# Attention scores in two PSUM tiles of two banks instead of one of four, with the order of all work made anew

## Chip, cores and metric

One core of a Trainium2 chip. The metric is device microseconds (us) of one launch. The kernel before was timed three times: 781.19, 783.55 and 784.84 us, median 783.55 us.

## What is computed

Causal attention in blocks of 64 (4 batches, 8 heads, 576 positions, head size 64), then two feed-forward layers over the 2304 tokens. Cut to what matters:

```
scores = scale * np.matmul(q, k.transpose(0, 1, 3, 2))
scores = np.where(block_i >= block_j, scores, -1e9)
attn = softmax(scores)
x = np.matmul(attn, v)                       # 2304 x 512 after the transpose of heads
h = x @ w_in;  g = np.maximum(h, 0.0) + np.log1p(np.exp(-np.abs(h)));  x = g @ w_out       # 512 -> 2048 -> 512
h = x @ w_in2; solu = h * softmax(h); x = layernorm(solu) * g_ln @ w_out2                  # 512 -> 1024 -> 512
```

## The kernel before

Each large product is made of three matmuls in a fast float type: both operands are split into a high and a low part, and high x high, high x low and low x high are added up in PSUM.

**The work comes in five kinds of items.** `UnitA` is attention for the first 256 queries of two heads (16 units, at the start). `UnitC` is attention from query 256 on for two heads (16 units, one after another; called a unit below). `Piece` converts weights. `Pair` takes two of the 16 column blocks of the first layer for 256 tokens: 24 matmuls into `hp` (tasks `a`), three ACT functions and a few DVE operations, then 24 matmuls into `acc` (tasks `b`). `Tok` is the second layer for 128 tokens. Pairs of one group of tokens run between the units of the next, so that PE has work while a unit waits for its softmax.

**The order is planned.** A unit's tasks are handed to `Plan.add` with an engine, a duration, a rank and the tasks that must come first. `Plan.run` goes through the plan's own time and gives each engine the ready task of lowest rank; the tables `OFF` and `RANK` are numbers added to the ranks. Tasks that two engines can do (`{"ACT": ..., "DVE": ...}`) go to the one that would end sooner. What comes out is one fixed list of instructions for each engine and for the DMA queue of SP; on the chip each engine takes its list in order.

**Two kinds of waits.** The plan's dependencies only set the order. The waits that the chip obeys are put in afterwards by the tile layer, which goes through that order and makes an access to a PSUM tile wait for the accesses of other engines to the same tile that stand before it, whether or not they touch the same banks.

**A unit's scores** lie in the tile `S`, four banks of 512 columns (line 821). `mm_both` writes the scores of 128 queries of both heads into banks 0 and 1 (i = 0, 384 keys) and of the next 128 into banks 2 and 3 (i = 1, 512 keys). DVE masks each half (`mask`, L467) and reduces it to its maxima (`max`, L472); ACT takes the exponentials head by head (`exp`, L481): twice into `eC0`, twice into `eC1`. Then `mm_qk(2)` writes the last 64 queries (576 keys, 288 columns a bank) into banks 0 and 1 again, and one more maximum and exponential follow. Each exponential is cut into 16-bit halves (`split`, tile `hl`), transposed by DMA (`tr`), and put together by DVE (`merge`, L522). The product with v (`pv`) of a unit runs in the middle of the next unit: `tail` puts it behind an exponential of that unit, into bank 3, which `exp(1, 1)`, the first of the two on `eC1`, has read out. `scale` (L538) multiplies it by the reciprocal sums, which come back from DRAM in `rC`. All matmuls stand at line 238.

```
mm01 = add("PE", 1614, 0.0, self.mm_both, [self.t_ql] + ...)
self.t_mm = t = add("PE", 797, r, partial(self.mm_qk, 2), [mm01, self.t_exp[0, 0], self.t_exp[0, 1]])
p1.tail([self.t_exp[1, 1]])
```

Of the kernel before, what the change touches and what calls it, by code (L numbers as in the profile page):

```python
# [10 lines left out]
F32 = mybir.dt.float32  # L11
# [9 lines left out]


OFF = {
    "Pair.a": -354.9, "Pair.abs": 39459.0, "Pair.b": 18236.7, "Pair.do_gh": 216226.0, "Pair.do_gl": 13257.7,
    "Pair.evac": -82948.2, "Pair.exp": -117702.0, "Pair.ln": -30665.3, "Pair.store": -79781.5, "Pair.stt": -62739.8,
    "Piece.bits0": -100434.0, "Piece.bits0@P0": -27714.9, "Piece.bits1": 65312.7, "Piece.bits1@P0": -101077.0,
    "Piece.do_hi": -19168.6, "Piece.do_hi@P0": -29991.6, "Piece.do_hi_g": -10835.1, "Piece.do_lo": 62401.8,
    "Piece.do_lo@P": -122217.0, "Piece.do_lo@P0": -16882.1, "Piece.do_lo_g": -33281.2, "Piece.load": 61438.7,
    "Piece.load@P0": -221951.0, "Piece.signed": -4876.1, "Piece.signed@P0": -103215.0, "Tok.a": -132718.0,
    "Tok.aggr": 7517.3, "Tok.bm": 58620.7, "Tok.center": -11408.7, "Tok.exp": -45235.8, "Tok.ln_hi": 28283.8,  # L30
    "Tok.ln_lo": 116041.0, "Tok.load": -268344.0, "Tok.logexp": -134098.0, "Tok.max": -65917.9,
    "Tok.merge": -135054.0, "Tok.mul": 52834.8, "Tok.o_evac": 47450.1, "Tok.small1": 71861.5, "Tok.small2": -55930.6,
    "Tok.split": -4685.6, "Tok.split_hi": 24778.5, "Tok.split_lo": -127140.0, "Tok.stats": 68934.5,
    "Tok.store": 157613.0, "Tok.tr": -45442.3, "Tok.x_hi": -107660.0, "Tok.x_lo": -20156.8, "UnitA.copy": -193390.0,
# [15 lines left out]
    "UnitC.den2": 65738.1, "UnitC.exp": 104667.0, "UnitC.load_qk": -83707.0, "UnitC.load_v": -36917.0,  # L50
    "UnitC.mask": -89564.7, "UnitC.max": -78960.5, "UnitC.merge": 54501.7, "UnitC.merge4": 149992.0,
    "UnitC.mm_both": -120396.0, "UnitC.mm_qk": -21356.3, "UnitC.norm": 76221.3, "UnitC.pv": -31503.3,
    "UnitC.qk_hi": -189467.0, "UnitC.qk_lo": -5389.2, "UnitC.rs_load": 138338.0, "UnitC.rs_store": -59470.7,
    "UnitC.scale": -44805.3, "UnitC.split": 94027.7, "UnitC.tr": -223984.0, "UnitC.x_hi": 131467.0,
    "UnitC.x_lo": 10651.6, "UnitC.xx": -154207.0,
}
RANK = {
# [3 lines left out]
    "Tok": (611105.0, 4133.14),  # L61
}
MARGIN = {
    "PE": 600.0, "ACT": 100.0, "DVE": 100.0, "POOL": 100.0,
# [2 lines left out]
B, H, S, D = 4, 8, 576, 64  # L67
# [4 lines left out]
NB = S - NA  # L72

QA = (slice(0, 128), slice(128, 384))
MASKED = -8.0e9
BANKS = (slice(0, 2), slice(2, 4), slice(0, 2))

WC = (384, 512, 576)

# [136 lines left out]
def dve_ns(n, per=1.04):  # L216
    return 70.0 + per * n
# [11 lines left out]
def body(ctx: ExitStack, tc: tile.TileContext, qk, qkA, vP, vA, w1, w2, u1, u2, gln, out):  # L229
    nc = tc.nc  # L230
    PE, ACT, DVE, POOL, SP = nc.tensor, nc.scalar, nc.vector, nc.gpsimd, nc.sync
# [5 lines left out]
    def mm(out, lhsT, rhs, start, stop):  # L237
        PE.matmul(out, lhsT, rhs, start=start, stop=stop, skip_group_check=True)  # L238
# [9 lines left out]
    def at_of(lst, i):  # L248
        return lst[i] if 0 <= i < len(lst) else None
# [16 lines left out]
    state = {}  # L266
# [90 lines left out]
    class UnitC:  # L357
# [6 lines left out]
        def plan(self, prev, opened):  # L364
            p1, p2 = at_of(prev, len(prev) - 1), at_of(prev, len(prev) - 2)
# [9 lines left out]
            for i, w in enumerate(WC):  # L375
                r, heads = 7.0 * i, ((0, 1), (1, 0), (0,))[i]
                if i < 2:
                    t = add("DVE", 140, r, partial(self.mask, i), [mm01])
                else:
                    self.t_mm = t = add("PE", 797, r, partial(self.mm_qk, 2), [mm01, self.t_exp[0, 0], self.t_exp[0, 1]])  # L380
                t = add("DVE", dve_ns(w * len(heads)), r, partial(self.max, i), [t])
                e = []
                for j in heads:
                    e.append(add("ACT", 250 + .833 * w, r, partial(self.exp, i, j), [t] + e + (p1.t_mg[i] if p1 else [])))
                    self.t_exp[i, j] = e[-1]
                if i == 1 and p1:
                    p1.tail([self.t_exp[1, 1]])
                cols, back = w * len(heads), [p1.t_tr[i]] if p1 else []
                n = [add({"ACT": 100 + .833 * cols, "DVE": 75 + .52 * cols}, None, r, partial(self.split, i, k), e + back) for k in range(2)]
                self.t_tr[i] = add("SP", 300 + 1.6 * cols, r, partial(self.tr, i), n, 2600.0)  # L390
# [54 lines left out]

        def scores(self, i):

            return state["S"][:, BANKS[i], 0:WC[i] if i < 2 else WC[2] // 2]

        def mm_qk(self, i):  # L450
            S, w = self.scores(i), WC[i]
# [74 lines left out]
            copy(e, state["p4"].bitcast(U16)[64 * j:64 * j + 64].rearrange("p (q two) -> p q two", two=2), src)  # L526

        def pv(self):
            o, ps = state["S"][:, 3], state["ps"]
            for t in range(4):  # L530
                q0 = 0 if t < 3 else 128
                for j in range(2):
                    mm(o[64 * j:64 * j + 64, q0:NB], self.v[:, 256 * j + 64 * t:256 * j + 64 * t + 64], ps[:, t, j, q0:NB], t == 0, False)
            mm(o[:, 256:NB], self.v[:, 512:640], state["p4"], False, True)

        def scale(self):
            self.xn = self.r
            DVE.tensor_mul(self.xn, state["S"][:, 3, 0:NB], self.r)  # L538

        def x_hi(self, c, off, done, w, e):  # L540
            copy(e, xt_of(c)[:, 0, self.pr, off:off + w], self.xn[:, done:done + w])
# [274 lines left out]
    def open_b():  # L816
        right[0].close()
        right[0] = ExitStack()
        state["pat"] = right[0].enter_context(pool("atB", "right"))
        q = right[0].enter_context(pool("qaB", "right", space=PSUM))  # L820
        state["S"] = q.tile([128, 4, 512], F32, name="S")
        state["dC"] = [[state["pat"].tile([128, 32], F32, name=f"d{x}{i}") for x in "CT"] for i in range(2)]
        for d, _ in state["dC"]:
            DVE.memset(d, 1.0)
        state["eC"] = [state["pat"].tile([128, 2 if i < 2 else 1, w], F32, name=f"eC{i}") for i, w in enumerate((WC[0], WC[1], WC[2] + 64))]
        state["hl"] = [state["pat"].tile([128, (2 * w if i < 2 else w + 64)], F32, name=f"hl{i}") for i, w in enumerate(WC)]
        DVE.memset(state["hl"][2], 0.0)
        state["ps"] = state["pat"].tile([128, 4, 2, NB], F32, name="ps")
        state["p4"] = state["pat"].tile([128, 64], F32, name="p4")
# [323 lines left out]
```

## Time and profile before

| | |
|---|---|
| median of three runs | 783.55 us |
| the profiled execution, and its span | 784.22 us, 782.4 us |
| mean granted PE clock | 0.985 of full |
| PE busy with matmuls | 735.1 us, 94% of the span |
| weight loads (beside matmuls) | 652.5 us, 83% |
| DVE, ACT, POOL busy | 592.7 us (76%), 409.8 us (52%), 0.7 us |
| DMA | 95.00 MB, 121 GB/s |

The profiled execution is 1.8 us longer than its span (what lies around the instructions) and 0.7 us over the median. Unless a text says otherwise, places are in us from the start of the span. The 16 units run from 191.9 us, the first matmul into `S`, to 464 us, the last; the units are numbered 0 to 15 by their start.

### The profile page before, as it was taken

How to read it: one execution, taken by the hardware profiler on the slowest of the kernel's cores; microseconds unless marked ns; L12 is line 12 of the kernel's file. 1: busy time of each engine (PE TensorE's matmuls, PEld its weight loads, DVE VectorE, ACT ScalarE, POOL GpSimd, SP SyncE). 2: the span in 40 equal slices, each digit the busy share in tenths (PEclk: the TensorE clock that was granted, in tenths of full speed). 3: DMA queues.
4: the chain of work that ended last, by engine and by line, in shares of the span. 5: the costliest groups of instructions: out<-in, count | busy, mean ns of one | idle time of the engine just before them, and what ended most of it. 6: DMA issues, size and time to landing. Idle time of an engine off the chain costs nothing.

```text
span 782.4 us, 13713 instructions
## 1 busy us (share of the span) xinstructions
PE 735.1 (94%) x5288; PEld 652.5 (83%) x5288; DVE 592.7 (76%) x1232; ACT 409.8 (52%) x877; POOL 0.7 (0%) x6
## 2 busy tenths in 40 slices
PE   7899999999898988898898899999999999999998
PEld 4688989999877777777887699999999888888887
DVE  6899995565777876777888755634698998989883
ACT  5787855563765666655665645543454342233231
POOL 0000000000000000000000000000000000000000
PEclk9899999999999998999999999999999999999999
DMA  7665742223666665566876552302513524443233
GB/s 258 197 196 182 227 149 68 69 42 88 138 135 148 138 165 123 116 132 134 172 148 132 101 138 81 124 13 72 200 52 82 141 76 108 95 108 88 59 83 80
DMA packets 165216, 95.00 MB, mean 121 GB/s; under 512 B 134816, under 2 KB 148384, under 8 KB 165152
## 3 DMA queue, kind: packets, MB, share of 16 engines
q1 hardware_dynamic: 165152, 94.14, 47.9%
q8 instruction: 41, 0.67, 0.3%
q14 instruction: 23, 0.19, 0.1%
HBM read 51.91 MB, written 9.70 MB: 79 GB/s over the span
## 4 chain that ended last, share of the span: by engine, by line
PE 64%; DVE 18%; ACT 10%; DMA 4%; issue 3%; SPq 0%; ACTq 0%; DVEq 0%
PE hp L238 14%; PE acc L238 13%; PE op L238 13%; PE h L238 13%; PE S L238 8%; ACT eC L481 5%; DVE mC L472 4%; DMA raw<-in_w_dram 3%; PE R L238 2%; DVE ps L522 2%; DVE a L315 1%; DVE t L769 1%; DVE mA L627 1%; PE r L238 1%; ACT eA L636 1%
## 5 line engine op out<-in xcount | busy, mean ns | idle before, releaser
L238 PE MATMUL hp<-xt,w 128*128 128x256 f32 x1728 | 216.6, 282 | 0.4 <-DVE t L769 0.3
L238 PEld LDWEIGHTS hp<-xt,w 128*128 128x128 f32 x1728 | 207.7, 190 | 6.9 <-issue 5.2
L238 PE MATMUL acc<-gh,w 128*128 128x256 f32 x768 | 144.8, 281 | 0.5 <-ACT gh L244 0.5
L238 PEld LDWEIGHTS acc<-gh,w 128*128 128x128 f32 x768 | 121.4, 189 | 3.0 <-issue 2.1
L238 PE MATMUL acc<-gl,w 128*128 128x256 f32 x384 | 107.6, 280 | 1.8 <-DVE gl L777 1.7
L238 PE MATMUL h<-u,w 128*128 128x512 f32 x432 | 100.2, 389 | 0.0
L238 PE MATMUL op<-w,w2w 128*128 128x512 f32 (+1 forms) x456 | 100.0, 378 | 0.0
L238 PEld LDWEIGHTS op<-w,w2w 128*128 128x128 f32 x456 | 82.5, 188 | 16.0
L238 PEld LDWEIGHTS h<-u,w 128*128 128x128 f32 x432 | 80.8, 188 | 16.6
L481 ACT ACTIVATE eC<-S,mC 128x384 f32<-128x384 f32 (+2 forms) x80 | 52.0, 653 | 61.0 <-DVE mC L472 26.9
L760 ACT ACTIVATE t<-hp 128x512 f32<-128x512 f32 x72 | 42.7, 593 | 66.1 <-PE hp L238 55.6
L769 DVE SCALAR_TENSOR_TENSOR t<-hp,t 128x512 f32<-128x512 f32 x72 | 49.1, 682 | 35.9 <-ACT t L766 35.5
L238 PEld LDWEIGHTS acc<-gl,w 128*128 128x128 f32 x384 | 72.1, 188 | 2.5 <-DVE gl L777 2.4
L238 PE MATMUL S<-ps,v 128*64 128x320 f32 (+1 forms) x256 | 38.8, 450 | 14.9 <-ACT eC L481 12.9
L1070 ACT ACTIVATE ob<-op,A 128x512 f32<-128x512 f32 (+1 forms) x19 | 12.6, 663 | 75.8 <-PE op L238 72.8
L777 DVE TENSOR_TENSOR gl<-t,gh 128x512 fp32r<-128x512 f32 x72 | 49.3, 684 | 2.0 <-ACT gh L244 0.7
L472 DVE TENSOR_REDUCE mC<-S 128x2 f32<-128x768 f32 (+2 forms) x48 | 45.4, 974 | 6.3 <-ACT eC L481 3.7
L238 PE MATMUL acc<-gh,w2w 128*128 128x256 f32 x256 | 48.4, 281 | 0.0
L766 ACT ACTIVATE t<-t 128x512 f32<-128x512 f32 x72 | 45.5, 632 | 1.4
L763 ACT ACTIVATE t<-t 128x512 f32<-128x512 f32 x72 | 45.6, 633 | 1.2
L522 DVE COPY ps<-eC 128x1536 uint16<-128x1536 uint16 (+2 forms) x48 | 45.2, 945 | 1.4 <-DMA eC<-hl 1.3
L238 PEld LDWEIGHTS S<-ps,v 128*64 128x64 f32 x256 | 18.5, 149 | 32.5 <-ACT eC L481 14.5
(175 smaller groups left out, 1086.0 us busy)
## 6 DMA issues: line engine op xcount, KB each, us to landing
raw<-in_w_dram SPq DMA_DIRECT2D x32, 512.0 KB, 4.7
qkC<-in_qk_dram SPq DMA_DIRECT2D x16, 480.0 KB
raw_u<-in_u_dram SPq DMA_DIRECT2D x11, 512.0 KB, 3.5
v<-in_vP_dram SPq DMA_DIRECT2D x16, 320.0 KB, 2.9
x2s<-stg SPq DMA_DIRECT2D x18, 256.0 KB, 2.8
xr<-x2s SPq DMA_DIRECT2D x18, 256.0 KB, 3.2
qkA<-in_qkA_dram SPq DMA_DIRECT2D x16, 256.0 KB, 4.0
out_dram<-ob SPq DMA_DIRECT2D x15, 256.0 KB, 2.2
```

Source lines behind the costliest of these rows:

```text
L238: PE.matmul(out, lhsT, rhs, start=start, stop=stop, skip_group_check=True)
L315: DVE.scalar_tensor_tensor(out=self.a, in0=self.raw[:, :, 0], scalar=29, in1=self.a, op0=ALU.logical_shift_right, op1=ALU.bitwise_or)
L472: DVE.tensor_reduce(out=self.m[:, i:4:2] if i < 2 else self.m[:, 4:5], in_=self.scores(i), axis=AX.X if i < 2 else AX.XY, op=ALU.max, nega ...
L481: ACT.activation(e, sc, AF.Exp, bias=self.m[:, c:c + 1], accum_out=self.den[:, d:d + 1])
L522: DVE.tensor_copy(dst, src)
L627: DVE.tensor_reduce(out=self.m[:, i, w * j:w * j + w], in_=st[:, :, QA[i]], axis=AX.X, op=ALU.max, negate=True)
L760: ACT.activation(self.t, self.hp, AF.Abs)
L763: ACT.activation(self.t, self.t, AF.Exp, scale=-1.0)
L766: ACT.activation(self.t, self.t, AF.Ln, bias=1.0)
L769: DVE.scalar_tensor_tensor(out=self.t, in0=self.hp, scalar=0.0, in1=self.t, op0=ALU.max, op1=ALU.add)
L777: DVE.tensor_sub(self.gl, self.t, self.gh)
L1070: ACT.activation(self.ob[:, cols], self.o[cols.start][:, cols], AF.Copy, scale=self.A)
```

## The change

The tile of four banks becomes a list of two tiles of two: scores i = 0 and 2 in `S0`, scores i = 1 and the product with v in `S1` (its second bank). The banks hold the same data as before. The product with v is put behind the last exponential on `S1`, `exp(1, 0)`, and not behind the first. All numbers of `OFF` and `RANK` are others, and so the order of the whole program is another. Units 8 to 15 of `UnitA` are transposed by DMA in both kernels.

```diff
 OFF = {
-    "Pair.a": -354.9, "Pair.abs": 39459.0, "Pair.b": 18236.7, "Pair.do_gh": 216226.0, "Pair.do_gl": 13257.7,
...
+    "Pair.a": 12428.5, "Pair.abs": -8234.6, "Pair.b": 41785.8, "Pair.do_gh": 285265.0, "Pair.do_gl": -45051.3,
...
-BANKS = (slice(0, 2), slice(2, 4), slice(0, 2))
...
                 if i == 1 and p1:
-                    p1.tail([self.t_exp[1, 1]])
+                    p1.tail([self.t_exp[1, 0]])
...
         def scores(self, i):
 
-            return state["S"][:, BANKS[i], 0:WC[i] if i < 2 else WC[2] // 2]
+            return state["S"][i % 2][:, :, 0:WC[i] if i < 2 else WC[2] // 2]
...
         def pv(self):
-            o, ps = state["S"][:, 3], state["ps"]
+            o, ps = state["S"][1][:, 1], state["ps"]
...
         def scale(self):
             self.xn = self.r
-            DVE.tensor_mul(self.xn, state["S"][:, 3, 0:NB], self.r)
+            DVE.tensor_mul(self.xn, state["S"][1][:, 1, 0:NB], self.r)
...
-        state["S"] = q.tile([128, 4, 512], F32, name="S")
+        state["S"] = [q.tile([128, 2, 512], F32, name=f"S{i}") for i in range(2)]
```

Two places of the order. PE in unit 11 (374.5 us in the trace), from the last matmul ahead of the product with v or the scores i = 2 on; `qkh` and `qkl` are the high and low parts of q and k, `ps` the transposed exponentials, `hp` a pair's tile. Before:

```order
L238 MATMUL acc_129<-gh_4172,w2_1_114 128x256
L238 MATMUL S_2315<-ps_2329,v_4274 64x320 x6
L238 MATMUL S_2315<-ps_2329,v_4274 64x192 x2
L238 MATMUL S_2315<-p4_2330,v_4274 128x64
L238 MATMUL S_2315<-qkh_4190 128x288 x2
L238 MATMUL S_2315<-qkl_4191,qkh_4190 128x288 x2
L238 MATMUL S_2315<-qkh_4190,qkl_4191 128x288 x2
L238 MATMUL hp0_130<-xt_2721,w1_8_105 128x256 x12
L238 MATMUL hp0_130<-xt_2721,w1_9_106 128x256 x12
```

And changed:

```order
L236 MATMUL acc_129<-gh_4173,w2_1_114 128x256
L236 MATMUL S0_2315<-qkh_4191 128x288 x2
L236 MATMUL S0_2315<-qkl_4192,qkh_4191 128x288 x2
L236 MATMUL S0_2315<-qkh_4191,qkl_4192 128x288 x2
L236 MATMUL S1_2316<-ps_2330,v_4253 64x320 x6
L236 MATMUL S1_2316<-ps_2330,v_4253 64x192 x2
L236 MATMUL S1_2316<-p4_2331,v_4253 128x64
L236 MATMUL hp0_130<-xt_2724,w1_8_105 128x256 x12
L236 MATMUL hp0_130<-xt_2724,w1_9_106 128x256 x12
```

The scores i = 2 moved ahead of the product with v. They stand in this order in all 15 units of the changed kernel that hold a product with v (unit 0 holds none); before, in 8 of the 15 (not in units 3, 8, 9, 11, 12, 14 and 15).

ACT in the same unit, from its first exponential on (`t` is a pair's tile, `hl` the halves for the transpose, `xt` the tokens for the pairs). Before:

```order
L481 ACTIVATE eC0_2322,dC1_2318<-S_2315,mC_4295 128x384 x2
L481 ACTIVATE eC1_2323,dC1_2318<-S_2315,mC_4295 128x512
L760 ACTIVATE t_4331<-hp1_131 128x512
L481 ACTIVATE eC1_2323,dC1_2318<-S_2315,mC_4295 128x512
L763 ACTIVATE t_4331<-t_4331 128x512
L244 ACTIVATE hl1_2326<-eC1_2323 128x1024
L766 ACTIVATE t_4331<-t_4331 128x512
L244 ACTIVATE xt_4049<-rC_4310 128x192
L481 ACTIVATE eC2_2324,dC1_2318<-S_2315,mC_4295 128x576
```

And changed:

```order
L479 ACTIVATE eC0_2323,dC1_2319<-S0_2315,mC_4296 128x384 x2
L479 ACTIVATE eC1_2324,dC1_2319<-S1_2316,mC_4296 128x512
L758 ACTIVATE t_4344<-hp1_131 128x512
L479 ACTIVATE eC1_2324,dC1_2319<-S1_2316,mC_4296 128x512
L761 ACTIVATE t_4344<-t_4344 128x512
L242 ACTIVATE hl1_2327<-eC1_2324 128x1024
L428 ACTIVATE qkh_4371<-qkC_4272 128x384
L429 ACTIVATE qkh_4371<-qkC_4272 128x576
L764 ACTIVATE t_4344<-t_4344 128x512
L479 ACTIVATE eC2_2325,dC1_2319<-S0_2315,mC_4296 128x576
```

The four exponentials stand as they stood; behind them the copies of the next q and k came to ACT, and the copy from `rC` went back behind the last exponential.

## Rows read from the trace of the kernel before

**Rows 1.** The page: span, and busy time of each engine.

```profile
span 782.4 us, 13713 instructions
PE 735.1 (94%) x5288; PEld 652.5 (83%) x5288; DVE 592.7 (76%) x1232; ACT 409.8 (52%) x877; POOL 0.7 (0%) x6
```

**Rows 2.** Busy time by stage; the columns stand in the first line.

```profile
core 0: us, PE busy (x) PEld busy (x) DVE busy (x) ACT busy (x) POOL busy (x), PEclk, DMA share, GB/s
60.00:190.00 130.00, 127.16 (x1087) 119.79 (x1088) 99.06 (x225) 81.98 (x183) 0.00 (x0) 1.00 0.40 117
190.00:466.00 276.00, 246.09 (x1931) 213.33 (x1930) 210.42 (x430) 167.51 (x369) 0.00 (x0) 0.97 0.64 138
466.00:720.00 254.00, 254.00 (x1599) 230.37 (x1599) 191.31 (x361) 101.52 (x180) 0.00 (x0) 1.00 0.35 93
```

**Rows 3.** Groups by shape, 190 to 466 us: busy, mean ns | idle before, releasers.

```profile
L238 PE MATMUL hp<-xt,w 128*128 128x256 f32 x672 | 86.1, 284 | 0.0
...
L238 PE MATMUL S<-ps,v 128*64 128x320 f32 x192 | 33.2, 485 | 14.9 <-ACT eC L481 12.9 <-DVE mC L472 1.9
...
L238 PE MATMUL S<-qkh 128*128 128x288 f32 x32 | 8.8, 357 | 14.7 <-ACT eC L481 14.7
...
L238 PE MATMUL S<-qkh 64*128 64x384 f32 x32 | 7.1, 441 | 0.4 <-DVE dC L487 0.4
```

**Rows 4.** Timeline of unit 11: start, us, engine, line [idle before <-releaser].

```profile
378.57 2.09 DVE L472 TENSOR_REDUCE mC<-S 128x2 f32<-128x768 f32 x2
...
380.75 0.58 ACT L481 ACTIVATE eC<-S,mC 128x384 f32<-128x384 f32 x1 [1.53 <-issue]
...
381.32 0.57 ACT L481 ACTIVATE eC<-S,mC 128x384 f32<-128x384 f32 x1
...
381.87 0.68 ACT L481 ACTIVATE eC<-S,mC 128x512 f32<-128x512 f32 x1
...
383.01 0.70 ACT L481 ACTIVATE eC<-S,mC 128x512 f32<-128x512 f32 x1
...
383.86 2.16 PE L238 MATMUL S<-ps,v 128*64 128x320 f32 x16 [1.97 <-ACT eC L481]
...
385.95 0.44 PE L238 MATMUL S<-p,v 128*128 128x64 f32 x2
...
386.19 0.51 PE L238 MATMUL S<-qkh 128*128 128x288 f32 x2
...
387.27 0.49 DVE L538 TENSOR_TENSOR rC<-S,rC 128x320 f32<-128x320 f32 x1 [0.76 <-PE S L238]
```

**Rows 5.** Groups by shape, 190 to 466 us: the first of a unit's maxima.

```profile
L472 DVE TENSOR_REDUCE mC<-S 128x2 f32<-128x768 f32 x16 | 15.3, 957 | 0.5
```

**Rows 6.** Timeline: the longest wait, unit 6, and two more, units 10 and 13.

```profile
293.37 0.58 ACT L481 ACTIVATE eC<-S,mC 128x384 f32<-128x384 f32 x1
...
296.01 0.85 PE L238 MATMUL S<-qkh 128*128 128x288 f32 x2 [4.00 <-ACT eC L481]
...
365.34 0.53 PE L238 MATMUL S<-qkh 128*128 128x288 f32 x2 [2.33 <-ACT eC L481]
...
415.17 0.53 PE L238 MATMUL S<-qkh 128*128 128x288 f32 x2 [2.34 <-ACT eC L481]
```

**Rows 7.** Busy time in the four stretches of low clock among the units.

```profile
247.10:250.40 3.30, 3.30 (x15) 1.68 (x12) 1.60 (x3) 1.14 (x2) 0.00 (x0) 0.50 1.02 191
294.90:301.60 6.70, 5.59 (x24) 4.77 (x26) 4.38 (x9) 4.36 (x8) 0.00 (x0) 0.50 0.35 63
332.40:335.70 3.30, 3.30 (x14) 1.54 (x16) 2.30 (x4) 1.84 (x3) 0.00 (x0) 0.50 0.87 164
366.60:369.80 3.20, 3.20 (x15) 2.42 (x15) 2.68 (x5) 2.54 (x5) 0.00 (x0) 0.50 0.66 123
```

**Rows 8.** Busy time: units 11 to 14, and DVE's densest stretch late on.

```profile
374.50:439.85 65.35, 57.78 (x469) 50.47 (x468) 53.19 (x110) 39.51 (x89) 0.00 (x0) 1.00 0.74 152
660.00:720.00 60.00, 60.00 (x267) 49.67 (x266) 54.48 (x105) 16.67 (x32) 0.00 (x0) 1.00 0.39 88
```

More of the change, by code (lines that the diff above doesn't have):

```diff
@@ L23 @@
 OFF = {
-    "Pair.a": -354.9, "Pair.abs": 39459.0, "Pair.b": 18236.7, "Pair.do_gh": 216226.0, "Pair.do_gl": 13257.7,
[L25 to L33, printed above, removed]
@@ L34 @@
-    "Tok.store": 157613.0, "Tok.tr": -45442.3, "Tok.x_hi": -107660.0, "Tok.x_lo": -20156.8, "UnitA.copy": -193390.0,
[15 rows of a table removed]
[L50 to L53, printed above, removed]
@@ L54 @@
-    "UnitC.scale": -44805.3, "UnitC.split": 94027.7, "UnitC.tr": -223984.0, "UnitC.x_hi": 131467.0,
-    "UnitC.x_lo": 10651.6, "UnitC.xx": -154207.0,
+    "Pair.a": 12428.5, "Pair.abs": -8234.6, "Pair.b": 41785.8, "Pair.do_gh": 285265.0, "Pair.do_gl": -45051.3,
+    "Pair.evac": -173962.0, "Pair.exp": -158186.0, "Pair.ln": -86649.2, "Pair.store": -88213.6, "Pair.stt": -80558.6,
+    "Piece.bits0": -149484.0, "Piece.bits0@P0": 9809.1, "Piece.bits1": 6393.7, "Piece.bits1@P0": -45964.6,
+    "Piece.do_hi": -30023.6, "Piece.do_hi@P0": -74774.0, "Piece.do_hi_g": -31706.7, "Piece.do_lo": 40606.2,
@@ new lines @@
+    "Piece.do_lo@P": -121157.0, "Piece.do_lo@P0": 3232.9, "Piece.do_lo_g": 15158.0, "Piece.load": 94950.2,
+    "Piece.load@P0": -223515.0, "Piece.signed": -24484.1, "Piece.signed@P0": -153609.0, "Tok.a": -169360.0,
+    "Tok.aggr": 29550.5, "Tok.bm": 66017.0, "Tok.center": -73694.2, "Tok.exp": -22151.4, "Tok.ln_hi": -29203.5,
+    "Tok.ln_lo": 130818.0, "Tok.load": -237142.0, "Tok.logexp": -7543.6, "Tok.max": -98271.9, "Tok.merge": -274577.0,
+    "Tok.mul": 83660.0, "Tok.o_evac": -22431.3, "Tok.small1": 60071.2, "Tok.small2": -9791.0, "Tok.split": -13386.5,
@@ new lines @@
+    "Tok.split_hi": 93221.1, "Tok.split_lo": -202895.0, "Tok.stats": 82349.8, "Tok.store": 131806.0,
+    "Tok.tr": 47009.0, "Tok.x_hi": -151871.0, "Tok.x_lo": 75364.2, "UnitA.copy": -231982.0, "UnitA.copy@A0": 90477.8,
[15 rows of a table added]
+    "UnitC.load_qk": 63685.7, "UnitC.load_v": -22826.8, "UnitC.mask": -29208.4, "UnitC.max": -18127.7,
+    "UnitC.merge": 52306.9, "UnitC.merge4": 157937.0, "UnitC.mm_both": -124870.0, "UnitC.mm_qk": 23695.7,
+    "UnitC.norm": 101436.0, "UnitC.pv": -47977.0, "UnitC.qk_hi": -38976.1, "UnitC.qk_lo": 25039.3,
@@ L56 @@
+    "UnitC.rs_load": 175002.0, "UnitC.rs_store": -56992.8, "UnitC.scale": -51298.9, "UnitC.split": 80698.7,
+    "UnitC.tr": -166472.0, "UnitC.x_hi": 78826.6, "UnitC.x_lo": -37546.0, "UnitC.xx": -286501.0,
 }
 RANK = {
[3 rows of a table removed]
-    "Tok": (611105.0, 4133.14),
[4 rows of a table added]
 }
```

37 rows, old and new, of tables (OFF, RANK) are left out of this document.

## The prediction

> **What bounds the kernel now.** I read the page first, then busy time by stage, then the groups of PE instructions by shape inside the stage that stood out, then single units in the timeline.
>
> PE is busy 94% of the span, and no other engine over 76% [rows 1]. The stages differ. From 60 to 190 us PE stands still for 2.8 us of 130, and from 466 to 720 us for none. Among the attention units, 190 to 466 us, it stands still for 276.0 - 246.1 = 29.9 us [rows 2]. So the kernel is bound by PE's own work except among the units, where PE waits.
>
> For what? The groups by shape account for all of it: 14.9 us ahead of the product with v, 14.7 us ahead of the scores i = 2, 0.4 us ahead of the scores i = 0, and none ahead of pairs' matmuls, such as those into `hp` [rows 3]. Nearly all of it was ended by an exponential (L481). So the stage loses its time in one loop: scores, maxima, exponentials, next scores.
>
> Unit 11 shows the loop [rows 4]. DVE takes both maxima in one go, 2.09 us from 378.57, to 380.66. Only then does ACT take the first exponential, at 380.75, though its maximum was ready after 0.96 us [rows 5]; the second maximum reads other banks. That is a wait for the tile. PE gets to the product with v at 383.86 - 1.97 = 381.89, where the second exponential ends too, and waits for the fourth (383.01 + 0.70). The scores i = 2, which need only the first two, stand behind it.
>
> **The low clock.** Four stretches among the units ran at half of full speed, 1.2 GHz in place of 2.4 [rows 7]. Those from 294.9 and 366.6 us on begin in or behind waits of 4.00 and 2.33 us, but the wait of 2.34 us that ended at 415.17 brought none [rows 6]. In them PE was busy for 3.30 + 5.59 + 3.30 + 3.20 = 15.4 us; at full clock this is half, so they cost 7.7 us. Waits and clock together, 29.9 + 7.7 = 37.6 us, are all that the units can give back.
>
> **Part 1: two tiles.** Three waits change, and no operation is added or removed.
> - The first exponential waits for its own maximum alone: earlier by the second one, 2.09 - 0.96 = 1.1 us. All four exponentials follow each other on ACT, so all come 1.1 us earlier, if nothing else holds ACT.
> - The scores i = 2 wait for the second exponential. Where they stood first, they waited for the third, or for one after work of a pair. From the end of the second to that of the third it is 382.55 - 381.89 = 0.66 us [rows 4]. So they may start 1.8 us earlier, and more where something stood between.
> - The product with v no longer waits for the maximum of i = 2 behind which it stood (1.9 of the 14.9 us) [rows 3].
>
> What is left of the waits? The longest, 4.00 us, was ended at 296.01; the second exponential of that unit ended at 293.95, in future at 292.9, and PE arrives at 292.0. This leaves 0.9 us, and gives 3.1. The two of 2.3 us leave 2.3 - 1.8 = 0.5 us each [rows 6]. The other six ahead of the scores i = 2 share 14.7 - 8.7 = 6.0 us, 1.0 us each, and go. Some 2 us of 14.7 are left.
>
> **Part 2: the scores i = 2 ahead of the product with v**, in the seven units where they stood behind it. Unit 11: PE arrives at 381.89 and the second exponential will end at 380.8, so the scores i = 2 run at once. They took from 386.19 to about 387.2, some 1.0 us, so PE is at the product with v at 382.9; the fourth exponential ends at 383.71 - 1.1 = 382.6 [rows 4]. No wait is left of 1.97 us. This order takes up to 1.0 + 1.1 = 2.1 us from each of the seven. Exponentials ended 12.9 us ahead of the product with v [rows 3], in eight waits, 1.6 us each on average; an estimate of 0.5 us is left, for the longer ones. The maxima's 1.9 us there were waits for the tile; I leave 0.4 us for them, and all of the 0.4 ahead of the scores i = 0.
>
> So 2.0 + 0.5 + 0.8 = 3.3 us of the 29.9 stay by this count.
>
> **Part 3: the wait that is added.** The product with v must now wait for both exponentials on `S1`. Behind it on PE stand the pairs and the next scores. The second of the two is the fourth exponential, which is counted above.
>
> **Part 4: the new order elsewhere.** Among the units there stand 1272 of the pairs' matmuls in place of 1320. The 48 go behind the units; at 86.1 / 672 = 0.13 us each [rows 3] they move 6 us of work from one place on PE to another, where PE never stands still [rows 2]: nothing in the sum. Copies trade engines (26 copies of `p4` on ACT in place of 21, 9 of the large `hl` on DVE in place of 13, 14 of the small in place of 7); DVE has 420 instructions there in place of 425. In the first stage PE takes one unit's scores 24 matmuls earlier, twelve matmuls into `acc` earlier and one product with v earlier; its 2.8 us of waits bound that on both sides. Past the units DVE and ACT change places, and SP issues the stores of group 5 a few places later, under a PE that is 100% busy. I cost all this at nothing; if that cover were gone, DVE with 191.3 of 254 us [rows 2] would be late next.
>
> **What is late next among the units: DVE.** It is busy for 210.4 us of 276 there [rows 2]. With some 26 us less for the stage that is 84%, and more in units 7 to 15, which now hold 72 of the pairs' matmuls each (units 11 to 14 before: 81 on average). The trace does not price this. The nearest rows are the stage before, with DVE at 76% and 2.8 us lost of 130, 2.2%, and the stretch from 660 us, with DVE at 54.5 / 60 = 91% and nothing lost [rows 2, 8]. I take 2.2% of 240 us, 5 us, as the shorter distances between engines there are like those of the units; the ends are 0 and, if DVE sets the pace, about 20 (the first rival).
>
> **The sum.** Waits: 29.9 - 3.3 - 5 = 21.6 us gone. Clock: waits over 2 us brought the low stretches, and hardly any are left; I keep one stretch, 1.7 us, so 6.0 us gone. Together 27.6. The profiled execution took 784.2 us, so 756.6; the median is 0.7 lower: **756 us**.
>
> **A rule against this.** The waits come back in every unit at the same two places of PE, with the pairs' matmuls in between free of them [rows 3]. The Trainium skill, Perfetto Trace Analysis, section Optimization Strategy, says that such consistent bubbles on the engine that should be saturated can mean too little PSUM for the next tile. The change gives no bank more, so by that rule alone the 29.9 us would stay and the sum would be 784. The rows speak against it where they show PE held by exponentials on other banks; it is the second rival.
>
> **Rivals.**
> - **DVE sets the pace.** In units 11 to 14 DVE was busy for 53.2 us of 65.35, 13.3 a unit, with PE at 14.4 [rows 8]. With nine matmuls less, 1.2 us, PE needs 13.2 us, and DVE would have to run without a break. At 91% busy [rows 8] it takes up to 13.3 / 0.91 = 14.6 us; as the pairs take some of its work along, I put it at 1 us a unit more than PE needs, 16 us in all. With 3.3 left and two low stretches, 18 us are saved: 766, between 762 and 775. Against it: busy time counts the tails of operations that overlap the next when the queue is full.
> - **The room was the limit.** Scores i = 0 and 2 still share two banks, and scores i = 1 and the product with v the other two. If PE only comes to wait one step later in the same loop, the time stays: 779 to 786. For it: the bubbles repeat. Against it: unit 11, where no bank that the exponential needs was taken.
> - **The product with v is late for the next scores: slower.** The next scores i = 1 now wait for `scale` on a product that comes later in the unit. In half of the units only 24 matmuls (3.1 us) and the scores i = 0 (0.7 us) stand between. `scale` ended at 387.76, 1.4 us after the product's end at 386.39 [rows 4], so it has 2.4 us to spare. It decides if `scale` ends over 3.8 us after the product. Behind half a unit of DVE's work, 6.6 us, it would hold PE for 2.8 us; in 16 units 45 us, against 28 saved: 800.
> - **Everything comes back**, waits and clock: 784 - 37.6 = 746 us.
>
> **How the numbers follow.** The forecast, 748 to 764 us, gets 0.62. DVE's pace gets 0.18, room 0.08, slower 0.06, and all of it back 0.06. The range from 747 to 772 holds the forecast, most of the first rival and a little of the last. A measurement of this kernel can tell 0.5%, 3.9 us, from no change. Faster than 779.6: 0.62 + 0.18 + 0.06 and 0.01 of the second rival, 0.87; within: 0.07; slower: 0.06.
>
> **What would show it.** Right: PE's idle time from the first scores to the last product with v is under 12 us; in a unit the first exponential starts before the second maximum ends; no wait of over 2 us ahead of scores i = 2, and at most one stretch of low clock. Wrong: waits of 1 us a unit that DVE ends (its pace), or that exponentials still end (room), or waits ahead of 128x512 score matmuls that `scale` ends (slower). It would also be wrong if PE stands still past the units.

## The result, and the profile after

The changed kernel takes **742.80 us** (median of 6 runs, 740.09 to 743.64), the kernel before beside it 782.52 us (6 runs, 781.12 to 784.84): a ratio of 0.949, 95% interval 0.946 to 0.951. The forecast was 756 us, with a range from 747 to 772. The direction was right, the gain was 40 us and not 28, and the time lies 4 us below the range. The last rival, waits and clock all back, came nearest: it put 746 us and was given 0.06.

The page of the changed kernel answers to [rows 1]. Its execution took 742.09 us, 42.1 less than that of the kernel before.

```profile
span 740.2 us, 13733 instructions
...
PE 721.4 (97%) x5288; PEld 643.9 (87%) x5288; DVE 586.7 (79%) x1223; ACT 413.4 (56%) x886; POOL 0.7 (0%) x6
```

Busy time by stage, with the columns of [rows 2]; the units now run from 192.3 to 419.5 us.

```profile
60.00:190.00 130.00, 127.35 (x1089) 119.82 (x1088) 99.18 (x226) 81.39 (x182) 0.00 (x0) 1.00 0.41 117
190.00:430.00 240.00, 239.15 (x1962) 211.38 (x1961) 209.40 (x433) 168.25 (x374) 0.00 (x0) 1.00 0.75 161
430.00:680.00 250.00, 250.00 (x1581) 226.01 (x1580) 188.83 (x356) 106.75 (x188) 0.00 (x0) 1.00 0.34 94
```

Among the units PE stands still for 0.85 us in place of 29.9, with DVE busy for 209.4 of 240 us, 87%. The clock is full throughout (1.00, before 0.97): none of the low stretches of [rows 7] has a successor there. The stages ahead and behind are as they were: PE stands still for 2.65 of 130 us in the one (before 2.84), and for none in the other.

The groups by shape, 190 to 430 us, answer to [rows 3].

```profile
L236 PE MATMUL hp<-xt,w 128*128 128x256 f32 x693 | 87.4, 280 | 0.0
...
L236 PE MATMUL S<-ps,v 128*64 128x320 f32 x192 | 29.4, 441 | 0.4 <-ACT eC L479 0.2
...
L236 PE MATMUL S<-qkh 64*128 64x384 f32 x32 | 7.1, 440 | 0.0
L236 PE MATMUL S<-qkh 128*128 128x288 f32 x32 | 7.0, 301 | 0.5 <-ACT eC L479 0.5
```

Ahead of the product with v 0.4 us are left of 14.9, ahead of the scores i = 2 0.5 of 14.7, ahead of the scores i = 0 nothing. No DVE instruction has taken the place of the exponentials as what ends PE's waits.

Unit 11 in the timeline, as [rows 4] show it for the kernel before:

```profile
348.60 0.30 DVE L465 MEMSET S<- 64x128 f32 x2
...
348.82 2.06 DVE L470 TENSOR_REDUCE mC<-S 128x2 f32<-128x768 f32 x2
...
349.84 0.58 ACT L479 ACTIVATE eC<-S,mC 128x384 f32<-128x384 f32 x1 [0.72 <-PE hp L236]
...
350.41 0.57 ACT L479 ACTIVATE eC<-S,mC 128x384 f32<-128x384 f32 x1
...
350.97 0.69 ACT L479 ACTIVATE eC<-S,mC 128x512 f32<-128x512 f32 x1
...
351.79 0.43 PE L236 MATMUL S<-qkh 128*128 128x288 f32 x2
...
352.13 0.69 ACT L479 ACTIVATE eC<-S,mC 128x512 f32<-128x512 f32 x1
...
352.96 2.16 PE L236 MATMUL S<-ps,v 128*64 128x320 f32 x16 [0.21 <-ACT eC L479]
```

The first exponential starts 1.02 us after the two maxima do; before, it was 2.18 us. The scores i = 2 run at 351.79, as soon as PE gets to them: the third exponential, the first on `S1`, has just ended (350.97 + 0.69 = 351.66), and the fourth is still to come. The product with v waits for 0.21 us in place of 1.97.

One more view shows what the prediction had not looked at: the exponentials by shape, in the kernel before (190 to 466 us).

```profile
L481 ACT ACTIVATE eC<-S,mC 128x512 f32<-128x512 f32 x32 | 21.9, 686 | 4.4 <-PE S L238 4.4
L481 ACT ACTIVATE eC<-S,mC 128x384 f32<-128x384 f32 x32 | 18.4, 576 | 36.4 <-DVE mC L472 19.3 <-issue 15.3 <-PE hp L238 1.8
...
L481 ACT ACTIVATE eC<-S,mC 128x576 f32<-128x576 f32 x16 | 11.9, 742 | 20.1 <-PE S L238 12.6 <-DVE mC L472 7.6
```

The same in the changed kernel (190 to 430 us):

```profile
L479 ACT ACTIVATE eC<-S,mC 128x512 f32<-128x512 f32 x32 | 21.9, 686 | 0.0
...
L479 ACT ACTIVATE eC<-S,mC 128x384 f32<-128x384 f32 x32 | 18.4, 577 | 24.3 <-DVE mC L470 14.0 <-issue 5.9 <-PE hp L236 4.4
...
L479 ACT ACTIVATE eC<-S,mC 128x576 f32<-128x576 f32 x16 | 11.7, 733 | 1.1 <-DVE p L244 0.6 <-DVE mC L470 0.5
```

In the kernel before, ACT too stood still in front of `S`, for 4.4 + 12.6 = 17.0 us until PE had finished writing there. The scores that it was to read had long been written; what it waited for were the scores i = 2 (ahead of the exponentials of 512 columns) or the product with v (ahead of those of 576), on the other half of the tile. This is gone as well.

DVE stood still there too. The multiplication by the sums (`scale`) waited in seven places, the seven units in which the scores i = 2 stand between the product with v and it. DVE's row of waits in the kernel before (line, releaser: us, times, longest):

```profile
DVE rC L538 <- PE S L238: 14.2, 7, 2.7
```

And in the changed kernel, where it waits for the product with v alone:

```profile
DVE rC L536 <- PE S L236: 2.9, 5, 1.3
```

One word on reading these rows: `issue` means that the profile names no releaser. All six such waits of the kernel before (15.3 us) ended 0.08 to 0.09 us behind the end of a second maximum, as in [rows 4] (378.57 + 2.09 = 380.66, then 380.75).

### The profile page after: what moved, and what is told of

It is laid out like the page before. It is cut to its first block, busy times and chain, and to the rows that moved or that the text cites. A ratio compares the mean times of both kernels' runs of the same rounds, so it can differ in the third digit from the quotient of the medians.

```text
span 740.2 us, 13733 instructions
## 1 busy us (share of the span) xinstructions
PE 721.4 (97%) x5288; PEld 643.9 (87%) x5288; DVE 586.7 (79%) x1223; ACT 413.4 (56%) x886; POOL 0.7 (0%) x6
## 4 chain that ended last, share of the span: by engine, by line
PE 56%; DMA 2%; ACT 1%; DVE 1%; issue 0%
PE op L236 13%; PE h L236 13%; PE acc L236 13%; PE hp L236 12%; PE S L236 5%; DMA eC<-hl 2%; ACT eC L479 1%; DVE mC L470 0%; ACT hl L242 0%; DVE ps L520 0%; ACT t L758 0%; DVE t L767 0%; DVE S L465 0%; DVE gl L775 0%; ACT ob L1068 0%
## 5 line engine op out<-in xcount | busy, mean ns | idle before, releaser
L236 PE MATMUL hp<-xt,w 128*128 128x256 f32 x1728 | 214.3, 280 | 0.2 <-DVE t L767 0.2
L236 PEld LDWEIGHTS hp<-xt,w 128*128 128x128 f32 x1728 | 204.3, 188 | 7.4 <-issue 6.4
L236 PE MATMUL acc<-gh,w 128*128 128x256 f32 x768 | 142.8, 280 | 0.5 <-ACT gh L242 0.5
L236 PEld LDWEIGHTS h<-u,w 128*128 128x128 f32 x432 | 80.8, 188 | 16.5
L479 ACT ACTIVATE eC<-S,mC 128x384 f32<-128x384 f32 (+2 forms) x80 | 51.9, 652 | 25.4 <-DVE mC L470 14.5
L1068 ACT ACTIVATE ob<-op,A 128x512 f32<-128x512 f32 (+1 forms) x19 | 12.6, 662 | 60.3 <-PE op L236 57.3
L242 ACT ACTIVATE hl<-eC 128x1024 uint16<-128x1024 uint16 (+2 forms) x48 | 41.7, 884 | 0.5
L236 PEld LDWEIGHTS acc<-gh,w2w 128*128 128x128 f32 x256 | 40.4, 189 | 0.8 <-issue 0.7
```

Of the source, the lines that this page charges most:

```text
L242: ACT.activation(out, a, AF.Copy)
L479: ACT.activation(e, sc, AF.Exp, bias=self.m[:, c:c + 1], accum_out=self.den[:, d:d + 1])
L1068: ACT.activation(self.ob[:, cols], self.o[cols.start][:, cols], AF.Copy, scale=self.A)
```

## The experiments

Each ran beside the kernel before (783.2 to 784.1 us in the three jobs); ratios have their 95% intervals. "Idle" is PE's standing still among the units, "low" the time of half clock there, both from the profiled execution.

| | median us | ratio | idle us | low us |
|---|---|---|---|---|
| before | 783.99 | 1 | 29.9 | 17.1 |
| changed (before beside it: 782.52) | 742.80 | 0.949 (0.946 to 0.951) | 0.85 | 0 |
| e1: two tiles, old order | 743.89 | 0.949 (0.948 to 0.951) | 1.4 | 0 |
| e2: one tile, new order | 788.57 | 1.006 (1.004 to 1.008) | 32.3 | 13.7 |
| e3: changed, DVE + 15 us | 748.62 | 0.956 (0.954 to 0.958) | 5.0 | 0 |
| e4: changed, DVE + 45 us | 777.49 | 0.992 (0.989 to 0.994) | 21.7 | 20.5 |
| e5: e1, exponential behind both maxima | 754.66 | 0.964 (0.962 to 0.966) | 8.8 | 0 |
| e6: e1, scores i = 2 behind exponentials on `S1` | 747.71 | 0.954 (0.952 to 0.956) | 3.4 | 0 |
| e7: e1, the three waits that were counted | 766.67 | 0.978 (0.973 to 0.982) | 17.9 | 6.8 |
| e8: e1, three that were not | 752.95 | 0.960 (0.956 to 0.965) | 9.4 | 0 |
| e9: e1, all six | 785.60 | 1.003 (1.001 to 1.005) | 35.0 | 10.2 |
| e10: reads of e9, no waits | 747.74 | 0.953 (0.950 to 0.957) | 3.5 | 0 |

**e1 and e2: which part of the change did it?** e1 is the kernel before, in its own order, with only the tile split:

```diff
-BANKS = (slice(0, 2), slice(2, 4), slice(0, 2))
-            return state["S"][:, BANKS[i], 0:WC[i] if i < 2 else WC[2] // 2]
+            return state["S"][i % 2][:, :, 0:WC[i] if i < 2 else WC[2] // 2]
...
-        state["S"] = q.tile([128, 4, 512], F32, name="S")
+        state["S"] = [q.tile([128, 2, 512], F32, name=f"S{i}") for i in range(2)]
```

> The kernel before with the tile of four banks cut into two of two and nothing else: every engine and the DMA queue have the order of before. If the waits for the whole tile held PE, they go here without a new order. By the working of the prediction the waits ahead of the scores i = 2 fall from 14.7 us to about 2, and those ahead of the product with v, which come 1.1 us earlier in seven units, from 14.9 to about 5; with the clock's 6 us this gives some 755 us. If the new order was needed for the gain, little is won: 775 us or more. On the size of the gain two theories: (a) a wait of PE costs about 0.16 us more than the idle time that the profile shows, because the matmul ahead of it is drawn with its 0.28 us and not with the 0.12 us at which the next would have started; then the time saved exceeds idle time and half of the low clock saved by 0.16 us for each wait that is gone, 3 to 5 us. (b) The excess came from the new order outside the units; then idle time and clock explain the saving of this run within 1.5 us.

e2 is the opposite: the changed kernel, all its order, with the tile of four banks.

> The changed kernel with one tile of four banks again: the new order, with the waits for the whole tile. If the tile is what counts, the waits are back: the product with v now stands behind the scores i = 2 in all units and waits for their maximum too, so 30 us or more of idle PE among the units and 780 to 795 us. If the order alone brought the gain, 745 to 760 us. Theory (a), a wait costs 0.16 us more than is shown: against the changed kernel the time grows by idle time, half of the low clock, and 4 to 6 us more. Theory (b), the excess lies in the order outside the units: as the order is the changed kernel's, idle time and clock explain the growth within 1.5 us.

The tile is the whole gain: e1 takes 743.89 us (743.66 to 744.10), faster than any theory had it. The new order without it is 4.6 us slower than before, and with it 1.1 us faster than e1, in another job and with intervals that overlap. The rows of PE's waits among the units (line, releaser: us, times, longest) in e1:

```profile
PE S L237 <- ACT eC L480: 1.4, 3, 0.8
```

And in e2, with those of ACT:

```profile
PE S L237 <- ACT eC L480: 29.7, 17, 2.6
...
ACT eC L480 <- PE S L237: 21.9, 17, 2.6
```

In e1 the scores i = 2 stand behind the product with v in seven units as before, and all of PE's idle time is 1.4 us. Both runs also speak on what a wait costs (idle time here is that of the whole span). e1's span is 40.2 us shorter than before, of which idle time makes 28.8 and half of the low clock's time 7.9; e2's is 43.8 longer than the changed kernel's, with 30.3 us more idle time and 6.6 for the clock. That leaves 3.5 and 6.9 us. Theory (b), that such a rest comes from the order elsewhere, is refuted: each run has the order of the kernel that it is compared with. Theory (a), 0.16 us more for each wait, makes 3.2 us in both, for the 20 waits that e1 lacks and the 20 that e2 has more: it covers e1 and half of e2. The other half of e2 stays open.

**e3 and e4: how near is DVE?** In the changed kernel the copy that puts transposed halves together is made twice: in e3 the first of a unit's (0.95 us more a unit), in e4 all (2.8 us).

```diff
         def merge(self, i):
...
+            DVE.tensor_copy(dst, src)
             DVE.tensor_copy(dst, src)
```

> The changed kernel with the first of the three copies that put a unit's transposed exponentials together done twice: 0.95 us more of DVE's work in each of 16 units, 15 us in all, the output unchanged. If DVE has room among the units, as operations that follow each other closely overlap, the time stays within 3 us of the changed kernel (742 to 746). If DVE sets the pace with its 209 us of 240, nearly all of the 15 us appear: 753 to 758 us.

> The changed kernel with all three of these copies done twice: 2.8 us more of DVE's work in each unit, 45 us in all. DVE has 240 - 209 = 31 us in which it is idle among the units, so here it must become the bound or nearly so. If it has room for about 3 us a unit, the time grows by 5 to 20 us, to 748 to 763 us, and PE's new waits are ended by DVE. If DVE set the pace already, it grows by 40 us or more, to 782.

15 us more of DVE cost 5.8 us of time, and 45 us cost 34.7. Both times lie between the two theories of their run: DVE was near its limit in the changed kernel, but not at it. Busy time from 190 to 420 us in the changed kernel and in e3, with the columns of [rows 2]:

```profile
190.00:420.00 230.00, 229.15 (x1874) 201.38 (x1873) 203.93 (x422) 164.88 (x368) 0.00 (x0) 1.00 0.77 164
```

```profile
190.00:420.00 230.00, 225.19 (x1832) 197.49 (x1830) 215.38 (x434) 160.85 (x362) 0.00 (x0) 1.00 0.78 158
```

And in e4, with its rows of waits:

```profile
190.00:420.00 230.00, 211.13 (x1641) 182.96 (x1641) 220.53 (x419) 147.30 (x330) 0.00 (x0) 0.97 0.69 145
...
ACT eC L479 <- issue: 24.4, 10, 5.1
ACT eC L479 <- DVE mC L470: 21.9, 9, 4.3
...
PE S L236 <- ACT eC L479: 16.9, 16, 2.7
```

DVE is busy for 94% and 96% of the stretch, where the changed kernel has 89%. Note by which row a late DVE shows on PE: 16.9 of e4's 21.7 us are waits for an exponential, and 4.3 us name DVE. The exponentials in turn waited for their maxima, by name in nine places; of the ten marked `issue`, eight ended 0.08 us behind the end of a maximum.

**e5 and e6: which of the waits?** Both are e1 with one wait put back, by a tiny operation that reads what the kernel before had to wait for. In e5 the first exponential waits for both maxima:

```diff
         def max(self, i):
...
+            if i == 1:
+                DVE.tensor_copy(self.m[:, 0:1], self.m[:, 0:1])
```

> Two tiles in the order of the kernel before (743.9 us), with one of the waits that the two tiles took away put back: the first exponential waits for both maxima again. For this DVE copies one column of maxima onto itself behind the maximum of i = 1 (some 0.1 us a unit, 2 us in all), and the first exponential reads that column. Nothing else differs; the scores i = 2 still need only the first two exponentials. Theory P (the prediction's split by unit: all exponentials come 1.1 us later again, so the 12.9 us ahead of the product with v stay, and of the 14.7 us ahead of the scores i = 2 some 8 stay): PE stands still for about 21 us among the units, 764 to 774 us. Rival Q (the loop is tight: any one of the waits put back brings nearly all of the idle time back): 776 us or more, 27 us idle or more. Rival R (the late exponentials alone were hidden by the pairs' work; what counted was that the scores i = 2 waited for an exponential on the other half): 750 us or less, under 6 us idle.

In e6 the scores i = 2 wait for the exponentials on `S1`:

```diff
             ACT.activation(e, sc, AF.Exp, bias=self.m[:, c:c + 1], accum_out=self.den[:, d:d + 1])
+            if i == 1:
+                ACT.activation(state["spare"], state["S"][0][:, 0, 0:1], AF.Copy)
```

> Two tiles in the order of the kernel before (743.9 us), with the other wait put back: behind each exponential of i = 1 ACT copies one element of S0 into a spare column (some 0.2 us each, 32 in all), so that the scores i = 2, which overwrite S0, wait again for the exponentials on S1 that stand ahead of them. The first exponential starts behind its own maximum. Theory P (the exponentials come 1.1 us earlier than in the kernel before, so of the nine waits ahead of the scores i = 2 about 14.7 - 9 x 1.1 = 5 us stay, and about 5 us ahead of the product with v): 10 us idle among the units, 752 to 760 us. Rival Q (any one wait put back brings nearly all back): 776 us or more. Rival R (this wait was the main one): 765 us or more, with 20 us idle or more, most of it ahead of the scores i = 2.

They cost 10.8 and 3.8 us over e1, the added operations included (e6's 32 reads were not tried without their wait). No theory had it: 754.7 lies between P and R, 747.7 under all of them, and the two make 14.6 us where 40 had to be explained. So the list of waits was short, or they cost more together than one by one. Going through what the kernel before waits for gave three more: the exponentials on `S1` behind the scores i = 2, and that of i = 2 behind the product with v (the 17.0 us above); the mask and the maximum of i = 0 behind the scores i = 1; and the multiplication by the sums behind the scores i = 2.

**e7 to e10: the waits in groups.** e7 has those that the prediction counted (both of the above, and the product with v behind the maximum of i = 2), e8 the three others, e9 all six. e10 has all the added operations of e9, but they read a spare column and so wait for nothing. The edit of e9 over e1:

```diff
         def mask(self, i):
+            if i == 0:
+                DVE.tensor_copy(state["seenD"], state["S"][1][:, 1, 0:1])
...
         def max(self, i):
...
+            if i == 1:
+                DVE.tensor_copy(self.m[:, 0:1], self.m[:, 0:1])
+            if i == 2:
+                DVE.tensor_copy(state["seenD"], state["S"][1][:, 1, 0:1])
...
         def exp(self, i, j):
...
+            if i > 0:
+                ACT.activation(state["seenA"], state["S"][0][:, 0, 0:1] if i == 1 else state["S"][1][:, 1, 0:1], AF.Copy)
             ACT.activation(e, sc, AF.Exp, bias=self.m[:, c:c + 1], accum_out=self.den[:, d:d + 1])
+            if i == 1:
+                ACT.activation(state["seenA"], state["S"][0][:, 0, 0:1], AF.Copy)
...
         def scale(self):
             self.xn = self.r
+            DVE.tensor_copy(state["seenD"], state["S"][0][:, 0, 0:1])
```

> Two tiles in the order of the kernel before, with the three waits that the prediction counted put back together: the first exponential waits for both maxima (as in e5), the scores i = 2 for the exponentials on S1 ahead of them (as in e6), and the product with v for the maximum of i = 2 (DVE copies one element of S1's second bank behind that maximum). e5 and e6 alone cost 10.8 and 3.8 us over two tiles in the old order (743.9). Theory C (these three are the whole account, as the prediction had it, and they add up to more together than one by one): 776 us or more, PE still for 25 us or more among the units. Theory L (six waits lie on one loop PE - DVE - ACT - PE, of which the prediction saw three; the pairs' work hides the first microseconds, so half of the waits cost less than half): 758 to 770 us. Theory M (the other three are the main ones): 758 us or less, about the sum of e5 and e6.

> Two tiles in the order of the kernel before, with the three waits put back that the prediction did not see: the exponentials on S1 wait for the scores i = 2 where these stand ahead of them, and the exponential of i = 2 for the product with v (ACT reads one element of the other tile ahead of each, some 0.17 us, 48 in all); the mask and the maximum of i = 0 wait for the scores i = 1 too, 0.7 us later; the multiplication by the sums waits for the scores i = 2 where these stand ahead of it (DVE reads one element of the other tile, some 0.14 us, 32 in all). Theory C: 750 us or less. Theory L: 750 to 765 us, and the gains lost in e7 and here together are less than the 40 us of all six. Theory M: 770 us or more, PE still for 20 us or more among the units.

> Two tiles in the order of the kernel before, with all six waits of e7 and e8 put back: every wait that the one tile of four banks made. If these waits are the whole effect of the one tile, the time is that of the kernel before (784 us) or a few microseconds more for the added reads: 782 to 792 us, PE still for some 30 us among the units and low clock there again. Under 775 us would mean that something else of the one tile costs time.

> The control for e9: the same added operations on DVE and ACT in the same places, but each reads a spare column of its own engine and so waits for nothing. 64 on DVE of 0.14 us (9 us; at the 0.38 us of time for each us that e3 showed, 3.5 us) and 80 on ACT of 0.17 us (14 us, an engine with 56% busy): 745 to 751 us in all theories. Over 755 us would mean that e7 to e9 measure the added operations more than the waits.

e9 gives back the whole gain: two tiles with all six waits take 785.6 us, 1.003 of the kernel before, and the added operations alone 3.9 us over e1 (e10). So the six waits together make the effect of the one tile on the time, to within these 4 us. The split is not quite the same: 35.0 us idle and 10.2 low in e9, 29.9 and 17.1 in the kernel before. Over e1, the counted three cost 22.8 us, the others 9.1, all six 41.7: 10 us more than the groups apart, of which 9.1 are idle time (33.6 us over e1, against 16.5 and 8.0). That is theory L. It also means that no share of the gain belongs to one wait alone. PE's waits among the units in e9:

```profile
PE S L237 <- ACT seenA L490: 30.6, 16, 3.3
```

In e10:

```profile
PE S L237 <- ACT eC L488: 3.4, 7, 0.8
```

In e7:

```profile
PE S L237 <- ACT seenA L486: 16.5, 13, 3.3
```

And in e8 those of ACT and PE:

```profile
ACT seenA L483 <- PE S L237: 8.6, 10, 1.4
...
PE S L237 <- ACT eC L484: 6.2, 7, 1.2
PE S L237 <- ACT seenA L483: 3.2, 4, 1.7
```

Lines 486 and 490 are the reads behind the exponentials on `S1`, line 483 the read ahead of an exponential, and 479, 480, 484 and 488 are the exponentials. The groups are not quite apart: e8's read ahead of an exponential on `S1` also holds PE (the 3.2 us of the last row). So what exists only together is, if anything, more than 10 us. It fits with work of the pairs that hides the first part of a delay; how much it hides in each unit was not tried.

## Why the prediction was too slow

The mechanism was right: PE was held by exponentials on banks that it did not need, and the split freed it. All that the prediction named as signs of being right came: 0.85 us of idle time (under 12), a first exponential ahead of the second maximum's end (349.84, and 348.82 + 2.06 = 350.88), no wait over 2 us, no low stretch. What failed were terms of the sum, which fell short by 42.1 - 27.6 = 14.5 us of the profiled executions, term by term:

- **"What is late next: DVE", 5 us kept. Measured: nothing.** Of the terms that were kept back this is the largest. The rate of 2.2% came from the stage before, whose waits are another code's. All of PE's waits among the units come to 0.85 us and none names DVE, and units 4, 5, 7, 13 and 14 took 13.24 us from scores to scores, the 13.2 that PE needs by the working of the first rival. e3 shows that at 87% a us of DVE costs 0.4 us, so the worry had ground, but it is a price on added work, not a loss that was there.
- **Waits: 3.3 us kept. Measured: 0.85.** Exponentials came 1.16 us earlier in unit 11 (1.02 against 2.18 us after the maxima's start), as Part 1 said with 1.1. But Part 1 named three of six waits. It read only PE's idle time; the 17.0 us that ACT stood still until PE had written, and DVE's 14.2, were in the same trace, one view away.
- **Clock: one low stretch kept, 1.7 us. Measured: none.** The longest wait left is 0.50 us. That waits over 2 us are what brings low clock, as the term had it, did not hold in the other runs (last section).
- **The ceiling of 37.6 us did not hold.** The idle time that is gone is 29.1 us and the clock's part 7.7, in all 36.8; the saving was 42.1. This step, that waits and clock are all there is to give back, weighs as much as the first: with nothing kept back, the sum would still have ended at 746 us. A part of the other 5.3 us are waits that the rows don't show as idle. A matmul is drawn longer than the step to the next one, so the start of every wait lies under the drawn tail of the matmul ahead of it. PE ahead of the longest wait of e9, in the timeline:

```profile
290.11 0.28 PE L237 MATMUL acc<-gl,w 128*128 128x256 f32 x1
290.23 0.28 PE L237 MATMUL acc<-gh,w 128*128 128x256 f32 x1
293.82 0.54 PE L237 MATMUL S<-qkh 128*128 128x288 f32 x2 [3.31 <-ACT seenA L490]
```

The first is drawn 0.28 us long, and the next starts 0.12 us after it. By that step the third would have started at 290.35; it was late by 3.47 us, and 3.31 are shown. With 19 waits gone (23 before, 4 after, the shortest counted too), 0.16 each make 3.0 of the 5.3 us, an estimate. In e9 against e10, a span 38.4 us longer is 30.6 of idle time, 4.9 of clock and 2.9 for 16 more waits, 0.18 each. The rest, some 2 us, was not settled.

**Part 2** gave the new order of PE up to 2.1 us in each of seven units. e1 keeps the old order there and gains all the same, so that credit was wrong: with the tile split the exponentials came so much earlier that the old order cost nothing that shows. Unit 11 in e1:

```profile
342.62 0.45 PE L237 MATMUL S<-qkh 64*128 64x384 f32 x2
...
345.13 2.06 DVE L471 TENSOR_REDUCE mC<-S 128x2 f32<-128x768 f32 x2
...
349.17 0.70 ACT L480 ACTIVATE eC<-S,mC 128x512 f32<-128x512 f32 x1
...
350.01 2.16 PE L237 MATMUL S<-ps,v 128*64 128x320 f32 x16 [0.24 <-ACT eC L480]
```

The unit's first matmul in the kernel before:

```profile
374.53 0.45 PE L238 MATMUL S<-qkh 64*128 64x384 f32 x2
```

Counted from that matmul, the fourth exponential ends after 7.25 us, before after 9.18 [rows 4], and DVE starts the maxima after 2.51 us, before after 4.04. So 1.5 of the 1.9 us come from a DVE that is less late, and only the rest from an exponential that no longer waits for the second maximum. Over the seven units the fourth exponential ends 1.75 us earlier on average and the maxima start 1.0 us earlier. Part 1 counted 1.1 us from the second maximum, of which some 0.75 came in these units, and did not count that DVE itself would come earlier. What of this is due to which of DVE's own waits was not tried alone.

**Part 3**, the wait that is added, cost next to nothing: the 0.21 us above is its largest, 0.4 us are all ahead of the product with v. **Part 4**, the order elsewhere at nothing, holds within the 1.1 us between e1 and the changed kernel; alone the order was slower by 4.6 us (e2).

**The rivals.** The room was not the limit: the banks are the same in number and use, PE stands still for 0.85 us, and the bubbles came back in e9 with waits alone. So the Trainium skill's reading of repeating gaps as too little PSUM (Perfetto Trace Analysis, Optimization Strategy) did not apply here, though the page says no more than that they can mean it. The slower case did not come: no wait ahead of the scores i = 0 or i = 1 is left. DVE's pace is refuted for this kernel and came near in e4, which at 777 us is slower than that rival's 775. (Its 18 us saved left out its own two low stretches, 3.4 us: 37.6 - 16 - 3.3 - 3.4 make 15 us, and 769 in place of 766.) And "everything comes back" was no extreme case to be given 0.06: with the counted terms at their measured sizes it is the sum itself.

## What to carry to other kernels

When an engine waits for an operation on data that it does not touch, look for a tile that is larger than what depends on what, and list every pair of engines that meet in it, in both directions: here six waits lay on one loop, and the idle time of an engine that is not the bound (ACT, 17 us) was part of it. Waits on one loop don't add up: put back in two groups they cost 32 us, together 42; taken out of all six, the same groups give 33 us (e9 to e8) and 19 us (e9 to e7), 52 in sum where there are 42. So what one wait is worth depends on which others are left, and single experiments can't be summed. And a charge for "the next engine" should come from what that engine's added work costs, which a doubled operation measures in one run, not from the losses of another stage.

## What the runs showed of the hardware

Low clock did not follow from the length of a wait. In the kernel before, a wait of 2.23 us was followed by a low stretch at 332.4, and one of 2.34 was not [rows 6, 7].

```profile
332.31 3.85 PE L238 MATMUL S<-ps,v 128*64 128x320 f32 x16 [2.23 <-ACT eC L481]
```

In e9 seven waits were over 2.3 us. The four longest, 3.31, 2.57, 2.56 and 2.49 us, were followed by none, the other three, 2.48, 2.32 and 2.31 us, each by one. Busy time in e9 behind four of them, which ended at 293.8, 328.7, 362.2 and 431.4, with the columns of [rows 2]:

```profile
293.90:297.30 3.40, 2.86 (x22) 2.59 (x24) 2.11 (x6) 2.70 (x7) 0.00 (x0) 1.00 0.62 116
329.90:333.30 3.40, 3.40 (x17) 2.28 (x14) 1.20 (x2) 0.76 (x2) 0.00 (x0) 0.50 0.95 179
362.50:366.00 3.50, 2.92 (x24) 2.54 (x25) 2.71 (x6) 3.02 (x8) 0.00 (x0) 1.00 0.59 110
432.30:435.70 3.40, 3.40 (x17) 1.99 (x14) 1.47 (x3) 1.07 (x2) 0.00 (x0) 0.50 0.96 178
```

A granted 0.50 is 1.2 GHz, 1.00 is 2.4 GHz. Behind the two waits without a low stretch came the scores i = 2, as at 293.82 above; behind the two with one came the product with v. But the longest wait of the kernel before stood ahead of scores i = 2 and did bring low clock [rows 6, 7], and e9's wait of 2.49 us stood ahead of the product with v and brought none. So that is no rule, and what decides was not settled.

Short waits don't keep the clock up for certain either. In e5 and e8, where no wait was over 1.71 us, there was no low stretch among the units. In e4 one began at 341.8, where the waits just ahead were of 1.40 and 0.78 us:

```profile
339.56 0.53 PE L236 MATMUL S<-qkh 128*128 128x288 f32 x2 [1.40 <-ACT eC L479]
...
341.39 3.75 PE L236 MATMUL S<-ps,v 128*64 128x320 f32 x16 [0.78 <-ACT eC L479]
```

```profile
341.80:345.20 3.40, 3.40 (x17) 1.41 (x13) 3.22 (x6) 3.37 (x8) 0.00 (x0) 0.50 0.77 143
```
